# Attention and a gated feed-forward on one core: the high by high score products of two banks in the two halves of TensorE's rows

## The chip, the cores and the metric

The program runs on one core of a Trainium2 chip. The time is that of the device in microseconds for one execution of the whole program. A core has five engines that run their own queues: PE (TensorE, matmuls; its weight loads are shown apart as PEld), DVE (VectorE), ACT (ScalarE), POOL (GpSimd) and SP (SyncE, which here only issues DMAs). Matmuls write to banks of a separate memory (PSUM); one bank holds 512 columns of 32 bit for 128 rows.

## The reference

For 8 batches of 8 heads, 576 positions and 64 elements a head:

```python
scores = scale * np.matmul(q, k.transpose(0, 1, 3, 2))
cum = np.cumsum(np.maximum(s, 0.0), axis=-1)
bias = -(cum[:, :, :, None] - cum[:, :, None, :])
scores = np.where(causal, -1000000000.0, scores + np.minimum(bias, 0.0))
attn = softmax(scores)                      # with 1e-9 added to the sum
attn_out = np.matmul(attn, v)               # -> x: 4608 tokens x 512
gate = 1.0 / (1.0 + np.exp(-(x @ w_gate)))  # 512 x 1536
out = (gate * (x @ w_val)) @ w_out          # 1536 x 512
```

All inputs are 32 bit. The 64 (batch, head) pairs are called heads 0 to 63 below.

## The kernel before

**Split operands.** From head 8 on, and in the whole feed-forward, a 32 bit operand is split into a 16 bit high part and a 16 bit low part, and a product is made of matmuls of the parts. In the feed-forward that is three matmuls (high by high, high by low, low by high). Heads 0 to 7 are done with 32 bit matmuls (`n_prep`, `n_s`, `n_av`, `n_x`); these also contain the only matmuls of 64 rows, the transposes of a 64-row tile in `n_x` (line 628).

**The tile T of a head.** A head has 64 elements, so the two parts of q or k fill the 128 rows together. `split_qk` splits q and k, and one transposing DMA (line 394) writes `T[i]`, three planes of 576 columns: plane 0 has k's high part in rows 0 to 63 and its low part in rows 64 to 127, plane 1 the same of q. `swap_k` fills plane 2 by two DMAs on SP (lines 399 and 400): k's parts with the halves exchanged, low above and high below. There are three such tiles in turn.

**Scores.** A head's queries are cut into five tiles (`TILES`): tile 0 of 64 queries and tiles 1 to 4 of 128, which see 64, 192, 320, 448 and 576 keys. `s_part(i, t)` makes one tile's scores. Tile 4 takes two banks of 288 columns, the others one each: six banks a head. Per bank there are two matmuls of 128 rows with the same stationary operand, q's high and low part of the tile: with plane 0 (line 445) they give high by high plus low by low, with plane 2 (line 446) high by low plus low by high. `score_bank` gives out three banks in turn. DVE empties a bank in `max_part` (line 470, which adds the bias and takes the row minimum of the negated scores), ACT takes the exponential (line 473); POOL masks the bias row ahead of that (line 460).

**After the scores.** `p_part` splits the probabilities, a transposing DMA on SP turns them (line 493), `av_part` multiplies them by v, 40 matmuls a head of 64 or 65 columns (lines 505 to 510), two heads later; `x_part` and `split_x` make x of it, in 16 bit parts.

**The feed-forward.** It goes in 18 groups of 256 tokens by 12 blocks of 128 hidden columns. `ffn_in` makes one block: 24 matmuls of 256 columns (line 656; 48 smaller ones where the group lies across two batches). `ffn_out` adds it to the output: 6 matmuls of 512 columns (line 686).

**What sets the order.** A loop over ticks, five per head, calls these functions; a tick t of head i makes the scores of tile 4 - t, the mask and maximum of the tile before, and so on, and feed-forward blocks are set between by a quota. A scheduler that simulates the program's time then chooses the order of the instructions on each engine from this, the dependencies and the free buffers; some instructions (`pin`) are kept in the order in which they are written. From tick 90 on (head 18), `more_room` hands a large tile `t2big`, which shows as `t2f` in the profile, to a third T, second buffers for q and k and other things, under names in `spare`.

Of the kernel before, what the change touches and what calls it, by code (L numbers as in the profile page):

```python
# [7 lines left out]
F16 = mybir.dt.float16  # L8
# [8 lines left out]
P = 128  # L17
# [6 lines left out]
def tile_attention_then_gated_ffn(  # L24
# [11 lines left out]
    nc = tc.nc  # L36
    B, H, S, D = q.shape
# [7 lines left out]
    QC = S // QP  # L45

    TILES = [(0, 64, 64)] + [(64 + 128 * i, 128, 192 + 128 * i) for i in range(4)]
    NTL = len(TILES)
# [3 lines left out]
    PAD = NTL * P - S  # L52
# [11 lines left out]
    def score_bank(name):  # L64
        score["n"] += 1
        tag, bufs = ("x", 1) if score["n"] % 3 == 0 else ("s", 2)
        return pp.tile([P, 512], F32, tag=tag, name=name, bufs=bufs)
# [46 lines left out]
    def pin(ins):  # L114

        return tc.keep_in_program_order(ins) if spare else ins

    def first(now=True):
        return tc.high_priority(1000) if now else ExitStack()
# [84 lines left out]
    spare = {}  # L204

    def more_room():
        c = 0
        for name, n in (("qk16", QC * 2 * D), ("qk32", 4 * QC * D), ("T", 3 * S // 2), ("vsq0", S), ("vsq1", S)):
            spare[name] = t2big[:, c : c + n]
            c += n  # L210

# [2 lines left out]
    flat = w2all.rearrange("p f l n -> p (f l n)").bitcast(I32)  # L214
# [118 lines left out]
            out_scale(b)  # L333


    qk32, qkc, T, crow, v32, v16, vx, PT, xq, S_ps, rl, AV = {}, {}, {}, {}, {}, {}, {}, {}, {}, {}, {}, {}
    NG = (NT + GT - 1) // GT

    def load_qk(p):
# [58 lines left out]
    def swap_k(i):  # L398
        pin(nc.sync.dma_start(T[i][0:64, 2], T[i][64:128, 0]))
        pin(nc.sync.dma_start(T[i][64:128, 2], T[i][0:64, 0]))  # L400

    def load_crow(i):
        crow[i] = wp.tile([P, S], F32, tag="cr", name=f"cr{i}")
        if i > 0:
            nc.sync.dma_start(crow[i][0:1], cum_d[i : i + 1, :])
# [17 lines left out]
    def split_v(p):  # L423

        sc = sv[2 * p // H][0]
        t = wp.tile([P, 5, 2, 2 * D + 2], F16, tag="v16", name=f"v16_{p}")
        nc.gpsimd.memset(t[:, :, :, 2 * D :], 1.0)
        src = v32[p][:, :, :, 0:D]
        nc.scalar.activation(t[:, :, :, D : 2 * D], src, AF.Copy, scale=sc)
        nc.vector.scalar_tensor_tensor(t[:, :, :, 0:D], src, sc, t[:, :, :, D : 2 * D], ALU.mult, ALU.subtract)  # L430
        v16[p] = t

        vx[p] = v32[p].rearrange("p c h n -> p (c h n)").bitcast(F16).rearrange("p (c h n) -> p c h n", c=5, h=2)
        for g in range(2):
            nc.sync.dma_start(vx[p][64 * g : 64 * g + 64], t[:64])

    def s_part(i, t):
        w = TILES[t][2]
        c0 = S + t * P - PAD
        lhs = T[i].rearrange("p a n -> p (a n)")[:, c0 : c0 + P]  # L440
        pieces = [(0, w)] if w <= 512 else [(0, w // 2), (w // 2, w)]
        S_ps[i, t] = []
        for a, b_ in pieces:
            ps = score_bank(f"s{i}_{t}_{a}")
            nc.tensor.matmul(ps[:, : b_ - a], lhs, T[i][:, 0, a:b_], start=True, stop=False)  # L445
            nc.tensor.matmul(ps[:, : b_ - a], lhs, T[i][:, 2, a:b_], start=False, stop=True)  # L446
            S_ps[i, t].append((ps, a, b_))

    def bias_row(i):
        if i < NN:  # L450
            rl[i] = crow[i]
            return
        r = wp.tile([P, S], F32, tag="rl", name=f"rl{i}")
        nc.vector.tensor_scalar(r, crow[i], qkc[i // 2][1][:, 0:1], None, ALU.mult)
        rl[i] = r
# [112 lines left out]
    def n_s(i, t):  # L568
        q0, m, w = TILES[t]
        p, j = divmod(i, 2)  # L570
        nS[i, t] = []
        for a, b_ in [(0, w)] if w <= 512 else [(0, w // 2), (w // 2, w)]:
            ps = score_bank(f"s{i}_{t}_{a}")
            nc.tensor.matmul(ps[:, : b_ - a], qT[i][:, q0 : q0 + P], kT[p][:, a:b_], start=True, stop=True)
            nS[i, t].append((ps, a, b_))
# [146 lines left out]
    NE, NOFF = 44, 87  # L722
# [6 lines left out]
    for n in range(nticks + 12):  # L729
        if n == NTL * EARLY:  # L730
            more_room()
        i, t = divmod(n, NTL)
        if i < NN:
            with first():
                n_s(i, NTL - 1 - t)
                if t == 0:
                    bias_row(i)
        elif n < nticks:
            if t == 0:
                bias_row(i)  # L740
            with first(NE <= n < NOFF):
                s_part(i, NTL - 1 - t)
        if 2 <= n < nticks + 2:
            a, z = divmod(n - 2, NTL)
            if a < NN:
# [4 lines left out]
        if 1 <= n < nticks + 1:  # L750
            a, z = divmod(n - 1, NTL)
# [7 lines left out]
        if 3 <= n < 3 + NTL * NN:  # L759
            with first():  # L760
                a, z = divmod(n - 3, NTL)
# [11 lines left out]
        if i < NH:  # L773
            p, j = divmod(i, 2)
# [19 lines left out]
            if NN <= i and j == 0 and t == 0:  # L794
                split_v(p)
            if not spare:
# [9 lines left out]
                if t == 3 and NN - 1 <= i:  # L806
                    swap_k(i + 1)
            elif i <= EARLY + 1:
                if j == 0:
                    if t == 1:  # L810
                        split_qk(i + 1)
                    if t == 3:
                        swap_k(i + 1)
                        load_qk(p + 2)
                else:
                    if t == 0:
                        qk_square(p + 1)
                    if t == 1:
                        qk_scale(p + 1)
                    if t == 2:  # L820
                        split_qk(i + 1)
                    if t == 4:
                        swap_k(i + 1)
                        split_qk(i + 2)
                        load_qk(p + 3)
# [50 lines left out]
        if n >= NE and state["u"] < 2 * NF:  # L876
            fdone = min(NF, int((n - NE + 1) * FPT))
            while state["u"] < 2 * fdone:
                f = state["u"]
# [58 lines left out]
```

## Time and profile before

| | |
|---|---|
| median of 3 runs | 1164.59 us (1159.92 to 1169.75) |
| the profiled execution | 1161.21 us, of which the span from first to last instruction is 1159.4 us |
| PE | 1095.0 us busy, 11644 instructions |
| DVE, ACT, POOL | 775.0, 749.2 and 264.9 us busy |
| mean granted clock of PE | 0.979 |
| DMA | 157.62 MB, mean 136 GB/s |
| score matmuls of heads 8 to 63 start | from 110.8 to 973.4 us |
| head 19 starts its scores at | 285.1 us |

Times in rows of the profile are microseconds from the start of the span, durations of a single instruction in ns where the row says so. A row of the timeline has start, duration, engine, line, operation, names, the rows and columns of TensorE that a matmul uses (128\*128), the shape that it writes, the type and the count; neighbours of one line are merged into one row, which shows the form of the first. PE is the matmul side; the records of its matmuls overlap, since they are pipelined, so a matmul's duration is longer than the distance to the next one's start. `gv` and `o` are the feed-forward's banks, `s` the scores', `av` the attention output's, `na_ps`, `nt_ps`, `nx_ps`, `nq_ps` those of heads 0 to 7.

### The profile page before, as it was taken

What the parts mean: (1) busy time and instruction counts of PE and PEld (TensorE: products, weight loads), DVE (VectorE), ACT (ScalarE), POOL (GpSimd) and SP (SyncE); (2) the same over time, 40 slices, a digit from 0 to 9 for tenths busy, and PEclk for the clock granted to TensorE, in tenths of its full rate; (3) what the DMA queues carried; (4) which work ended last, traced back from release to release, by engine and by line L of the source; (5) the groups of instructions that cost most, each with busy time, mean ns of one, the idle gap of its engine ahead of it and who ended that gap; (6) DMA issues with size and microseconds to landing.
All of it is one profiled execution on the core that took longest, in us unless ns stands there. A gap on an engine that the chain in (4) does not pass through costs nothing.

```text
span 1159.4 us, 30337 instructions
## 1 busy us (share of the span) xinstructions
PE 1095.0 (94%) x11644; PEld 855.9 (74%) x11644; DVE 775.0 (67%) x2393; ACT 749.2 (65%) x1465; POOL 264.9 (23%) x570
## 2 busy tenths in 40 slices
PE   6786789989999999999999999999999999999997
PEld 5664677656777887778777777778877887787775
DVE  6888879785788777776566577777777775222221
ACT  6988667776777877676656577667777764233222
POOL 5535333231222222121111122222222221000000
PEclk9879899999999999999999999999999999999999
DMA  9675678898889797886737578877877764000000
GB/s 276 199 223 141 129 152 167 177 186 160 154 164 193 151 187 157 153 160 115 164 66 150 99 159 167 168 152 164 154 160 145 146 122 88 12 20 19 1 19 19
DMA packets 435886, 157.62 MB, mean 136 GB/s; under 512 B 403551, under 2 KB 423007, under 8 KB 435742
## 3 DMA queue, kind: packets, MB, share of 16 engines
q1 hardware_dynamic: 418398, 127.12, 57.1%
q10 hardware_dynamic: 13824, 16.78, 4.6%
q0 software_dynamic: 3520, 11.80, 3.1%
q8 instruction: 91, 1.49, 0.5%
q14 instruction: 53, 0.43, 0.1%
HBM read 56.92 MB, written 9.58 MB: 57 GB/s over the span
## 4 chain that ended last, share of the span: by engine, by line
PE 60%; issue 23%; DMA 5%; DVE 4%; ACT 3%; POOL 3%; SPq 1%; ACTq 0%; POOLq 0%; DVEq 0%
PE gv L656 33%; PE o L686 16%; PE s L446 3%; PE s L445 3%; DMA pt<-p 1%; PE av L505 1%; PE av L507 1%; PE av L506 1%; DMA T<-T 1%; POOL rl L460 1%; DMA T<-qk 1%; POOL cr L460 1%; PE na_ps L604 1%; DVE e L470 1%; DMA nqk<-in_q_dram 1%
## 5 line engine op out<-in xcount | busy, mean ns | idle before, releaser
L656 PE MATMUL gv<-x,w 128*128 128x256 f16 (+3 forms) x6912 | 614.9, 247 | 3.9 <-DVE t2f L663 2.3
L656 PEld LDWEIGHTS <-w 128*128 128x128 f16 x6912 | 535.1, 98 | 61.4 <-issue 4.6
L686 PE MATMUL o<-w2all,h 128*128 128x512 f16 x1296 | 314.8, 379 | 0.0
L460 POOL TENSOR_SCALAR_AFFINE_SELECT rl<-rl 128x64 f32<-128x64 f32 (+1 forms) x280 | 113.7, 407 | 512.0 <-DVE em L470 453.3
L473 ACT ACTIVATE e<-e,em 128x576 f32<-128x576 f32 x280 | 154.4, 554 | 88.0 <-DVE em L470 85.9
L661 ACT ACTIVATE th<-gv,scb 128x256 f32<-128x256 f32 (+3 forms) x288 | 111.3, 411 | 147.5 <-PE gv L656 142.5
L686 PEld LDWEIGHTS <-h 128*128 128x128 f16 x1296 | 123.4, 98 | 106.4
L663 DVE SCALAR_TENSOR_TENSOR t<-th,gv 128x256 f32<-128x256 f32 x192 | 80.0, 417 | 133.1 <-ACT th L661 131.9
L470 DVE CUSTOM_DVE_ANT_0 e<-s,rl,qkcf 128x288 f32<-128x288 f32 x280 | 135.7, 485 | 32.1 <-PE s L446 27.8
L671 ACT ACTIVATE h<-t,hsc 128x256 f16<-128x256 f32 x192 | 96.6, 503 | 80.4 <-DVE t L663 80.3
L482 DVE SCALAR_TENSOR_TENSOR p<-e,p 128x384 f16<-128x384 f32 x224 | 102.6, 498 | 41.0 <-ACT p L477 40.2
L672 DVE SCALAR_TENSOR_TENSOR h<-t,hsc,h 128x256 f16<-128x256 f32 x192 | 93.3, 486 | 43.4 <-ACT h L671 42.6
L477 ACT ACTIVATE p<-e 128x1152 f16<-128x1152 f32 x112 | 112.0, 1000 | 2.5
L505 PE MATMUL av<-v,pt 128*128 128x65 f16 x560 | 67.8, 193 | 5.3 <-DMA pt<-p 5.3
L446 PE MATMUL s<-T 128*128 128x288 f16 (+2 forms) x246 | 62.1, 279 | 11.3 <-DMA T<-T 11.3
L445 PE MATMUL s<-T 128*128 128x288 f16 (+2 forms) x246 | 64.4, 279 | 7.1 <-DMA T<-qk 4.2
L694 POOL DMA_DIRECT2D out_dram<-osb x36 | 20.4, 566 | 211.5 <-ACT osb L693 210.9
L507 PE MATMUL av<-v,pt 128*128 128x65 f16 x560 | 67.8, 194 | 0.0
L506 PE MATMUL av<-v,pt 128*128 128x64 f16 x560 | 67.7, 192 | 0.0
L505 PEld LDWEIGHTS <-pt 128*128 128x128 f16 x560 | 52.5, 98 | 11.0 <-DMA pt<-p 6.1
L408 POOL PARTITION_BROADCAST cr<-cr x63 | 58.5, 929 | 2.1 <-DMA cr<-cum_d 2.0
L506 PEld LDWEIGHTS <-pt 128*128 128x128 f16 x560 | 52.5, 97 | 4.9
(155 smaller groups left out, 1415.0 us busy)
## 6 DMA issues: line engine op xcount, KB each, us to landing
out_dram<-osb POOLq DMA_DIRECT2D x36, 256.0 KB, 2.8
v<-v SPq DMA_DIRECT2D x56, 162.5 KB
v<-in_v_dram SPq DMA_DIRECT2D x64, 128.0 KB
T<-T SPq DMA_DIRECT2D x82, 72.0 KB
t2f<-in_v_dram SPq DMA_DIRECT2D x20, 288.0 KB
qk<-in_q_dram SPq DMA_DIRECT2D x17, 288.0 KB
qk<-in_k_dram SPq DMA_DIRECT2D x17, 288.0 KB
w2all<-in_moe_w_gate_dram ACTq DMA_DIRECT2D x7, 512.0 KB
```

What stands on the lines that cost most here:

```text
L445: nc.tensor.matmul(ps[:, : b_ - a], lhs, T[i][:, 0, a:b_], start=True, stop=False)
L446: nc.tensor.matmul(ps[:, : b_ - a], lhs, T[i][:, 2, a:b_], start=False, stop=True)
L460: nc.gpsimd.affine_select(rl[i][:, q0:w], rl[i][:, q0:w], pattern=[[-1, m]], compare_op=ALU.is_ge, fill=-MASKED if i < NN else MASKED, bas ...
L470: nc.vector.tensor_tensor_reduce(e_t[t][:, a:b_], ps[:, : b_ - a], rl[i][:, a:b_], c, init, ALU.add, ALU.min, acc)
L473: nc.scalar.activation(e_t[t][:, :w], e_t[t][:, :w], AF.Exp, bias=init, scale=-1.0)
L477: nc.scalar.activation(p_s[h_][:, 0], e_s[h_], AF.Copy, scale=PSCALE)
L482: nc.vector.scalar_tensor_tensor(flat[:, LOW[t] * P : (LOW[t] + t) * P], e_t[t][:, : t * P], PSCALE, flat[:, kb * P : (kb + t) * P], ALU.m ...
L505: nc.tensor.matmul(AV[i][:, t], hi, v_[:, D : 2 * D + 1], start=kb == 0, stop=False)
L506: nc.tensor.matmul(AV[i][:, t, 0:D], hi, v_[:, 0:D], start=False, stop=False)
L656: nc.tensor.matmul(ps[:, gv, a:e], w1[f][:, cc, gv, wl], x_of(b, cc)[:, xl, c0 + a : c0 + e], start=(c == 0), stop=(c == 3 * NC - 1))
L661: nc.scalar.activation(th[:, a:e], ps[:, 0, a:e], AF.Tanh, scale=scb[b][:, f : f + 1])
L686: nc.tensor.matmul(ps[:m], h[:, hl, tt * P : tt * P + m], w2[f][:, wl], start=(f == 0 and c == 0), stop=(f == NF - 1 and c == 2))
```

## The change

From head 19 on (the first whose `swap_k` runs after `more_room`), the scores are made by a new function `s_pair` for two banks at a time.

* `swap_k` issues a third DMA on SP: it copies q's high part, plane 1 of rows 0 to 63 with the 64 columns before it (640 columns), to rows 64 to 127 of a tile `QD`, one of three in turn in `t2big`.
* `s_pair` takes two banks. The first gets high by high from rows 0 to 63 alone (q's high part and plane 0), the second from rows 64 to 127 alone (`QD` and plane 2, where k's high part lies below): two matmuls of 64 rows. Then each bank gets one matmul of 128 rows with plane 2, high by low plus low by high. The product low by low is left out for these heads. The number of matmuls stays at two per bank.
* The pairs are tile 4's two banks at tick 0 of a head, tiles 3 and 2 at tick 1, tiles 1 and 0 at tick 3. Mask and maximum keep their ticks.

```diff
-        for name, n in (("qk16", QC * 2 * D), ("qk32", 4 * QC * D), ("T", 3 * S // 2), ("vsq0", S), ("vsq1", S)):
+        for name, n in (("qk16", QC * 2 * D), ("qk32", 4 * QC * D), ("T", 3 * S // 2), ("vsq0", S), ("vsq1", S),
+                        ("qd0", NTL * P // 2), ("qd1", NTL * P // 2), ("qd2", NTL * P // 2)):
             spare[name] = t2big[:, c : c + n]
...
     def swap_k(i):
         pin(nc.sync.dma_start(T[i][0:64, 2], T[i][64:128, 0]))
         pin(nc.sync.dma_start(T[i][64:128, 2], T[i][0:64, 0]))
+        if spare:
+            QD[i] = spare[f"qd{i % 3}"].bitcast(F16)
+            pin(nc.sync.dma_start(QD[i][64:128], T[i].rearrange("p a n -> p (a n)")[0:64, S - PAD : 2 * S]))
...
+    def s_pair(i, tiles):
+
+        flat = T[i].rearrange("p a n -> p (a n)")
+        parts = []
+        for t in tiles:
+            w = TILES[t][2]
+            S_ps[i, t] = []
+            for a, b_ in [(0, w)] if w <= 512 else [(0, w // 2), (w // 2, w)]:
+                ps = score_bank(f"s{i}_{t}_{a}")
+                S_ps[i, t].append((ps, a, b_))
+                parts.append((t, ps, a, b_))
+        for g, (t, ps, a, b_) in enumerate(parts):
+            rows = slice(64 * g, 64 * g + 64)
+            lhs = QD[i][rows, t * P : (t + 1) * P] if g else flat[rows, S + t * P - PAD : S + (t + 1) * P - PAD]
+            nc.tensor.matmul(ps[:, : b_ - a], lhs, T[i][rows, 2 * g, a:b_], start=True, stop=False)
+        for t, ps, a, b_ in parts:
+            nc.tensor.matmul(ps[:, : b_ - a], flat[:, S + t * P - PAD : S + (t + 1) * P - PAD], T[i][:, 2, a:b_],
+                             start=False, stop=True)
...
-            with first(NE <= n < NOFF):
-                s_part(i, NTL - 1 - t)
+            if i not in QD:
+                with first(NE <= n < NOFF):
+                    s_part(i, NTL - 1 - t)
+            elif t in (0, 1, 3):
+                s_pair(i, {0: (4,), 1: (3, 2), 3: (1, 0)}[t])
```

In the changed kernel the 64-row matmul of `s_pair` is line 455 and the 128-row one line 457; the lines of the feed-forward are 679 and 709, of the value matmuls 528 and on. Three places of the order follow. In the names, `s45_4_288` is head 45's bank of tile 4 that starts at key 288, `t2f` holds QD.

PE, tile 4 of head 45, before:

```order
L686 MATMUL o9_1_11644<-w2all_78,h9_4_11707 128x512
L445 LDWEIGHTS T45_11591
L445 MATMUL s45_4_0_11981<-T45_11591 128x288
L446 LDWEIGHTS T45_11591
L446 MATMUL s45_4_0_11981<-T45_11591 128x288
L445 LDWEIGHTS T45_11591
L445 MATMUL s45_4_288_11984<-T45_11591 128x288
L446 LDWEIGHTS T45_11591
L446 MATMUL s45_4_288_11984<-T45_11591 128x288
L656 LDWEIGHTS w1_8_74
```

and now:

```order
L709 MATMUL o9_1_11670<-w2all_78,h9_4_11734 128x512
L455 LDWEIGHTS T45_11620
L455 MATMUL s45_4_0_12009<-T45_11620 128x288
L455 LDWEIGHTS t2f_135
L455 MATMUL s45_4_288_12010<-T45_11620,t2f_135 128x288
L457 LDWEIGHTS T45_11620
L457 MATMUL s45_4_0_12009<-T45_11620 128x288
L457 LDWEIGHTS T45_11620
L457 MATMUL s45_4_288_12010<-T45_11620 128x288
L679 LDWEIGHTS w1_8_74
```

The two first matmuls of the two banks now stand together as 64-row ones, between the same neighbours. PE, tiles 3 and 2 of head 45, before:

```order
L445 MATMUL s45_3_0_12034<-T45_11591 128x448
L446 LDWEIGHTS T45_11591
L446 MATMUL s45_3_0_12034<-T45_11591 128x448
L505 LDWEIGHTS pt1_43_11655
L505 MATMUL av43_12052<-v16_21_11212,pt1_43_11655 128x65
```

and now:

```order
L455 MATMUL s45_3_0_12062<-T45_11620 128x448
L455 LDWEIGHTS t2f_135
L455 MATMUL s45_2_0_12063<-T45_11620,t2f_135 128x320
L457 LDWEIGHTS T45_11620
L457 MATMUL s45_3_0_12062<-T45_11620 128x448
L457 LDWEIGHTS T45_11620
L457 MATMUL s45_2_0_12063<-T45_11620 128x320
L528 LDWEIGHTS pt1_43_11684
L528 MATMUL av43_12083<-v16_21_11237,pt1_43_11684 128x65
```

Tile 2, which stood behind the 40 value matmuls, now stands ahead of them beside tile 3. SP's queue around the swap for head 46, before:

```order
L394 DMA_TRANSPOSE T46_11874<-qk16_46_11869 128x12x96
L346 DMA t2f_135<-in_k_dram 96x12x64
L160 DMA t2f_135<-in_v_dram 128x576
L399 DMA T46_11874<-T46_11874 64x576
L400 DMA T46_11874<-T46_11874 64x576
L493 DMA_TRANSPOSE pt0_44_12042<-p16_0_81 128x9x128
```

and now:

```order
L395 DMA_TRANSPOSE T46_11901<-qk16_46_11896 128x12x96
L347 DMA t2f_135<-in_k_dram 96x12x64
L160 DMA t2f_135<-in_v_dram 128x576
L400 DMA T46_11901<-T46_11901 64x576
L401 DMA T46_11901<-T46_11901 64x576
L404 DMA t2f_135<-T46_11901 64x640
L516 DMA_TRANSPOSE pt0_44_12073<-p16_0_81 128x9x128
```

The copy to QD (L404) goes out behind the two swaps and ahead of the transpose of the probabilities of head 44; the rest of the queue keeps its order here.

More of the change, by code (lines that the diff above doesn't have):

```diff
@@ L333, in ffn_scale @@
             out_scale(b)
-    qk32, qkc, T, crow, v32, v16, vx, PT, xq, S_ps, rl, AV = {}, {}, {}, {}, {}, {}, {}, {}, {}, {}, {}, {}
+    qk32, qkc, T, crow, QD, v32, v16, vx, PT, xq, S_ps, rl, AV = {}, {}, {}, {}, {}, {}, {}, {}, {}, {}, {}, {}, {}
     NG = (NT + GT - 1) // GT
```

## The prediction

> **What bounds the kernel now.** I read the page first, then the windows, then the waits, then PE's own timeline in a head of the middle stretch.
>
> ```profile
> span 1159.4 us, 30337 instructions
> PE 1095.0 (94%) x11644; PEld 855.9 (74%) x11644; DVE 775.0 (67%) x2393; ACT 749.2 (65%) x1465; POOL 264.9 (23%) x570
> ...
> 270.00:390.00 120.00, 115.46 (x1417) 91.22 (x1416) 91.01 (x298) 86.35 (x175) 30.77 (x69) 1.00 0.84 166
> 390.00:974.00 584.00, 584.00 (x6803) 462.21 (x6801) 420.51 (x1366) 403.78 (x791) 125.23 (x301) 1.00 0.74 145
> 974.00:1159.00 185.00, 178.84 (x1702) 136.62 (x1700) 44.10 (x104) 52.69 (x113) 4.83 (x9) 0.99 0.08 20
> ```
>
> The last three rows are stretches: start and end, length, then busy time of PE, PEld, DVE, ACT and POOL, the granted clock, the DMA share and GB/s. PE is busy in all 584 us from 390 to 974 and in 115.46 of the 120 us before; the clock is full in both. Heads 19 to 63, the ones that change, have their score matmuls inside these two stretches. Of the other engines none is over 76% busy there (DVE, 91.01 of 120 us). So in this part a microsecond more on PE is a microsecond more of span, and one less is one less, but for 4.5 us of PE idle between 270 and 390, of which these waits are the most:
>
> ```profile
> PE s L446 <- DMA t2f<-t2f: 1.9, 1, 1.9
> PE s L446 <- DMA T<-T: 1.3, 1, 1.3
> PE s L445 <- DMA t2f<-qk: 0.9, 1, 0.9
> ```
>
> (Waiter, awaited, us in total, times, longest.) A busy PE says nothing of what one matmul costs, since they are pipelined; a matmul costs the time from its start to the next one's. For head 45:
>
> ```profile
> 703.83 0.29 PE L445 MATMUL s<-T 128*128 128x288 f16 x1
> 703.95 0.29 PE L446 MATMUL s<-T 128*128 128x288 f16 x1
> ...
> 704.32 2.78 PE L656 MATMUL gv<-x,w 128*128 128x256 f16 x24
> ...
> 708.23 0.35 PE L445 MATMUL s<-T 128*128 128x448 f16 x1
> 708.42 0.35 PE L446 MATMUL s<-T 128*128 128x448 f16 x1
> 709.82 0.30 PE L445 MATMUL s<-T 128*128 128x320 f16 x1
> 709.95 0.30 PE L446 MATMUL s<-T 128*128 128x320 f16 x1
> 710.09 2.78 PE L656 MATMUL gv<-x,w 128*128 128x256 f16 x24
> ...
> 714.00 0.25 PE L445 MATMUL s<-T 128*128 128x192 f16 x1
> ...
> 714.17 0.19 PE L445 MATMUL s<-T 128*128 128x64 f16 x1
> 714.20 0.19 PE L446 MATMUL s<-T 128*128 128x64 f16 x1
> ...
> 718.14 0.29 PE L445 MATMUL s<-T 128*128 128x288 f16 x1
> ```
>
> One of 288 columns costs 0.122 us (0.49 for four), of 448 0.19, of 320 0.135 (0.27 for two), of 192 0.085, of 64 0.03. Nothing waits; the next head starts 14.3 us later.
>
> **What the side-by-side halves save.** Before, two banks take four full matmuls. After, they take two of 64 rows, which use different rows of the array and different banks, and two full ones; the number of matmuls is the same. If the two halves run at the same time, a pair saves the shorter of its two: 0.122 in tile 4, 0.135 for tiles 3 and 2, 0.03 for tiles 1 and 0, together 0.287 us a head. The order of the changed program does not pair all of them. Counted over the whole of it, 40 pairs of 288 and 288, 38 of 448 and 320 and 43 of 192 and 64 stand back to back; 26 halves stand alone (18 in heads 19 to 24, 8 as tiles 3 and 2 of heads 26, 34, 50 and 58), and two halves in the same rows stand together once. What stands alone costs as much as the full matmul it replaces, since cost goes by columns. Saved: 40 x 0.122 + 38 x 0.135 + 43 x 0.03 = 4.9 + 5.1 + 1.3 = 11.3 us. No row of this trace has two 64-row matmuls in different halves, so the bounds are 11.3 (side by side) and 0 (one after the other). I take 11.3: no semaphore stands between the two and neither rows nor banks are shared.
>
> The Trainium skill ("TensorE: Matmul & The Clock Gate", part 3 on packing small matmuls) says that matmuls on distinct row groups start about 4 ns apart and run concurrently. No run here shows it yet.
>
> **What going into 64 rows and out again costs.** This is the term that decides. The kernel has four matmuls of 64 rows, the transposes of a 64-row tile (L628), among matmuls of 128 rows. Two of the four places, PE and then the weight loads:
>
> ```profile
> 76.13 0.50 PE L595 MATMUL nt_ps<-ident,e 128*128 128x128 f32 x3
> 76.46 1.00 PE L604 MATMUL na_ps<-v,p 128*128 128x65 f32 x8
> 77.19 0.28 PE L604 MATMUL na_ps<-v,p 128*128 128x65 f32 x1
> 77.40 0.64 PE L628 MATMUL nx_ps<-ident,nx 64*128 64x64 f32 x3
> 77.87 0.41 PE L557 MATMUL nq_ps<-ident,nqk 96*128 96x96 f32 x3
> 78.12 0.58 PE L604 MATMUL na_ps<-v,p 128*128 128x65 f32 x4
> ...
> 107.93 0.50 PE L595 MATMUL nt_ps<-ident,e 128*128 128x128 f32 x3
> 108.36 0.64 PE L628 MATMUL nx_ps<-ident,nx 64*128 64x64 f32 x3
> 108.83 0.33 PE L574 MATMUL s<-nk,nq 128*128 128x64 f32 x2
> ...
> 77.39 0.14 PEld L628 LDWEIGHTS nx_ps<-ident,nx 64*128 64x128 f32 x1
> 77.60 0.20 PEld L628 LDWEIGHTS nx_ps<-ident,nx 128*128 128x128 f32 x2
> ```
>
> Rows of one line are merged; the form shown is the first one's. (77.19 is the last of the eight from 76.46.) Three 128-column transposes of full rows take 0.33 us (76.13 to 76.46), 0.11 each. The group of L628 is one of 64 rows and 64 columns and two full ones: by columns it should take 0.055 + 0.22 = 0.275 us. It takes 0.47 in both places (77.40 to 77.87, 108.36 to 108.83): 0.195 too much. And it starts late: 0.21 after the last matmul before it (77.19) instead of about 0.11, and 0.43 after the start of three transposes (107.93) instead of 0.33: another 0.10. Its weights are loaded only at its own start (77.39), and the next full ones' only 0.2 us later (77.60), where elsewhere loads run ahead under the matmul before. So one excursion into 64 rows and back costs 0.10 + 0.195 = about 0.30 us. The 96-row transposes right behind it (77.87 to 78.12, 0.083 each) show no such gap: it is not the number of rows as such, but the 64-row tile.
>
> The Trainium skill ("TensorEngine Tiling (Array Packing)", key properties) says that a change of tiling mode, not of the tile alone, drains TensorE; it gives no length. The trace agrees, with 0.30 us there and back. This rule speaks against the change.
>
> For 16 bit operands a part of the 0.30 is smaller, the loads that stand open:
>
> ```profile
> L628 PEld LDWEIGHTS nx_ps<-ident,nx 64*128 64x128 f32 x1 | 0.1, 135 | 0.1
> L445 PEld LDWEIGHTS <-T 128*128 128x128 f16 x246 | 24.1, 98 | 19.0 <-DMA T<-qk 5.6
> ```
>
> A load is 135 ns there and 98 ns for scores (the mean, behind the busy time). Two open loads make 0.30 - 2 x 0.037 = 0.225; I take 0.22 us. The bounds: 0.30, all as in the 32 bit rows, and 0.195, as if one way cost nothing more. In the changed order PE goes into 64 rows 148 times (121 pairs, the mixed one, 26 alone). 148 x 0.22 = 32.6 us; bounds 28.9 and 44.4.
>
> **The rest of the change.** The order of tiles: tile 2 moves up beside tile 3, ahead of the 40 value matmuls, and tile 0 beside 1. A pair wants two banks at once, so PE may wait for DVE, which empties them; behind it would queue the feed-forward matmuls.
>
> ```profile
> 709.04 0.68 DVE L470 CUSTOM_DVE_ANT_0 e<-s,rl,qkcf 128x448 f32<-128x448 f32 x1
> 715.08 0.41 DVE L470 CUSTOM_DVE_ANT_0 e<-s,rl,qkcf 128x192 f32<-128x192 f32 x1
> ```
>
> With three banks in turn, tiles 1 and 0 (714.00) need tile 3's bank, emptied at 709.72, and the next head's tile 4 (718.14) needs tile 1's, emptied at 715.49: 4.3 and 2.6 us to spare. Cost nothing; without that cover, up to 0.68 us a pair.
>
> The copy of q's high part is 45 more DMAs, each on SP behind the two swaps:
>
> ```profile
> 704.55 0.47 SPq L399 DMA_DIRECT2D T<-T  x1
> 705.07 0.59 SPq L400 DMA_DIRECT2D T<-T  x1
> 705.83 1.31 SPq L493 DMA_TRANSPOSE pt<-p  x1
> ...
> 351.44 3.36 DMA T<-T
> ```
>
> A third issue like the second (0.59 us) would go out at 705.7 and land some 3.4 us later (the swap in the chain of waits), near 709.1; its head reads it at 718.14. The transpose behind it moves by 0.6 us and is needed for the value matmuls a head later. So it costs nothing in the middle. In heads 19 to 24, where PE waits for swaps now, it is between +3.6 us (six heads, 0.6 later each) and -4.5 us (the present idle takes up some of the added PE time). I take 0. ACT, DVE and POOL get no instruction more.
>
> **The sum.** -11.3 + 32.6 = +21.3 us. On the profiled execution (span 1159.4, time 1161.2) that is 1182.5; the median of the runs is 3.4 us above it, 1164.6, and gives 1185.9. I say 1185. The forecast's own range: +28.9 - 11.3 - 4.5 = +13.1 to +44.4 - 11.3 + 3.6 = +36.7, that is 1174 (low end, on the profiled execution) to 1201 (high end, on the median).
>
> **The rivals.** *Faster: 16 bit pays no switch.* Loads of 16 bit weights into the other tile run ahead as they do everywhere else, and only the 11.3 us are left: 1150 to 1153. The trace's four excursions are all of 32 bit, which speaks for it being possible; that the wait stands in the matmul's own start as well as in the load speaks against. It decides below 11.3 / 148 = 0.076 us an excursion. Chance 0.08. The Trainium skill's tiling page gives row tiling with two tiles up to 2x (theoretical speedup), which is this case. *A cheap switch* of 0.08 to 0.15 us, half of what the rows show: +0.5 to +10.9 us, 1165 to 1176. Chance 0.13. *It does not do what it says:* the halves run one after the other. Nothing saved: +28.9 to +44.4, 1194 to 1209, most likely 1197. Chance 0.12; no row speaks for it or against. The forecast has 0.67.
>
> The bound for a difference is 1%, 11.6 us; the three runs before are 0.85% apart. Faster 0.05 (most of the first rival), same 0.17 (the cheap switch and the rest of the first), slower 0.78. The range that leaves out the first rival, the lower half of the cheap switch and the top of the third is 1168 to 1207.
>
> **What would show it.** In the profile after: the time from the start of a score pair's first matmul in heads 27 to 63 to that of the feed-forward matmul behind it, now 0.49 us for tile 4, should be about 0.49 - 0.12 + 0.22 = 0.59, counted from the end of the stream before it; the head's period should go from 14.3 to about 14.7 us; the second half should start within some tens of ns of the first (if 0.12 us later, the third rival); the weight load of the first full matmul should start only after the halves have gone through, 0.1 us or more (if it starts with them, the first rival). PE should be as busy in its stretch, and the time from 974 to the end, with no scores in it, unchanged at 185 us. I am wrong if the period stays at 14.3 or falls, or if PE waits for banks or for the copy.

## The result and the profile after

The changed kernel takes 1184.8 us (median of 4 runs, 1177.14 to 1187.89) against 1167.17 us before (4 runs): a ratio of 1.015, 95% interval 1.0102 to 1.0197, so 12 to 23 us slower. 1185 was forecast, and slower by over 1%.

The page after, and two stretches, from the start of head 19's scores to the last scores and from there to the end:

```profile
span 1185.8 us, 30440 instructions
PE 1115.8 (94%) x11644; PEld 836.2 (71%) x11644; DVE 774.5 (65%) x2393; ACT 747.5 (63%) x1465; POOL 265.8 (22%) x570
...
292.80:1000.00 707.20, 703.83 (x8010) 522.23 (x8008) 502.36 (x1638) 478.70 (x945) 152.05 (x362) 1.00 0.77 150
1000.00:1186.00 186.00, 179.18 (x1706) 136.96 (x1703) 44.32 (x104) 52.90 (x114) 4.78 (x9) 0.99 0.07 20
```

PE is as full as before (703.83 of 707.20 us), DVE, ACT and POOL do the same work, and the feed-forward's tail after the last scores is unchanged at 186 us. So the time went into what PE does in heads 19 to 63. Where these start and how they follow, first before, then after:

```profile
285.10 0.29 PE L445 MATMUL s<-T 128*128 128x288 f16 x1
397.81 0.29 PE L445 MATMUL s<-T 128*128 128x288 f16 x1
...
292.84 0.29 PE L455 MATMUL s<-T 64*128 64x288 f16 x1
408.44 0.29 PE L455 MATMUL s<-T 64*128 64x288 f16 x1
```

These are the first score matmuls of heads 19 and 27. From head 19's to the end of the span it is 874.3 us before and 893.0 after: 18.7 us more. The other 7.7 us between the two profiled executions lie ahead of head 19, up to which PE's order of instructions is the same in both. They are variation from run to run: in the nine profiles of this study head 19 starts anywhere from 283.0 us (same_rows, below) to 295.3 (alone_64), and among these the three kernels without a copy to QD start it at 285.10 (before), 287.96 (alone_96) and 295.29 (alone_64).

Head 45 on PE: first the row ahead of its tile 4 before, then the rows after, with the weight loads of tile 4 (these answer to the rows from 703.83 on before):

```profile
702.53 1.46 PE L686 MATMUL o<-w2all,h 128*128 128x512 f16 x6
...
721.64 1.46 PE L709 MATMUL o<-w2all,h 128*128 128x512 f16 x6
723.03 0.29 PE L455 MATMUL s<-T 64*128 64x288 f16 x1
723.03 0.29 PE L455 MATMUL s<-T,t2f 64*128 64x288 f16 x1
723.26 0.42 PE L457 MATMUL s<-T 128*128 128x288 f16 x2
723.51 2.78 PE L679 MATMUL gv<-x,w 128*128 128x256 f16 x24
...
727.52 0.36 PE L455 MATMUL s<-T 64*128 64x448 f16 x1
727.53 0.31 PE L455 MATMUL s<-T,t2f 64*128 64x320 f16 x1
727.82 0.50 PE L457 MATMUL s<-T 128*128 128x448 f16 x2
...
733.38 0.25 PE L455 MATMUL s<-T 64*128 64x192 f16 x1
733.38 0.20 PE L455 MATMUL s<-T,t2f 64*128 64x64 f16 x1
733.56 0.28 PE L457 MATMUL s<-T 128*128 128x192 f16 x2
733.68 2.78 PE L679 MATMUL gv<-x,w 128*128 128x256 f16 x24
...
737.70 0.29 PE L455 MATMUL s<-T 64*128 64x288 f16 x1
...
723.02 0.09 PEld L455 LDWEIGHTS <-T 64*128 64x128 f16 x1 [0.42 <-issue]
723.03 0.09 PEld L455 LDWEIGHTS <-t2f 64*128 64x128 f16 x1
723.25 0.11 PEld L457 LDWEIGHTS <-T 128*128 128x128 f16 x2
```

The two halves of a pair start together. But the first starts 0.09 us late: six matmuls of 512 columns take 1.30 us (702.53 to 703.83 before), which ends at 722.94, and the halves start at 723.03. The full ones follow 0.23 us after the halves (723.26), where 288 columns take 0.12: 0.11 late. The two full ones then take 0.25 us (723.26 to 723.51) where two took 0.24 before: another 0.01. The weight loads show the same: those of the halves and of the full matmuls stand only at their own start, and not under the matmul before. The head lasts 14.67 us (723.03 to 737.70), against 14.32 before (703.83 to 718.14, which are rounded), 0.35 us more. "Busy" shows none of this, since a matmul's record runs on past its stream and covers the gap.

### The profile page after: what moved, and what is told of

Same layout as the page of the kernel before. It is cut to its first block, busy times and chain, and to the rows that moved or that the text cites. A ratio compares the mean times of both kernels' runs of the same rounds, so it can differ in the third digit from the quotient of the medians.

```text
span 1185.8 us, 30440 instructions
## 1 busy us (share of the span) xinstructions
PE 1115.8 (94%) x11644; PEld 836.2 (71%) x11644; DVE 774.5 (65%) x2393; ACT 747.5 (63%) x1465; POOL 265.8 (22%) x570
## 4 chain that ended last, share of the span: by engine, by line
PE 59%; issue 21%; DMA 7%; ACT 4%; DVE 4%; POOL 2%; SPq 2%; ACTq 0%; POOLq 0%; DVEq 0%
PE gv L679 31%; PE o L709 16%; PE s L457 4%; PE s L455 2%; DMA T<-qk 2%; DMA v<-in_v_dram 1%; DMA pt<-p 1%; PE av L528 1%; PE av L530 1%; PE av L529 1%; PE s L597 1%; POOL rl L483 1%; DVE e L493 1%; ACT w L292 1%; ACT e L609 1%
## 5 line engine op out<-in xcount | busy, mean ns | idle before, releaser
L493 DVE CUSTOM_DVE_ANT_0 e<-s,rl,qkcf 128x288 f32<-128x288 f32 x280 | 135.8, 485 | 36.3 <-PE s L469 12.7
L528 PEld LDWEIGHTS <-pt 128*128 128x128 f16 x560 | 52.5, 98 | 9.1 <-DMA pt<-p 4.7
L477 DVE TENSOR_SCALAR rl<-cr,qkcf 128x576 f32<-128x576 f32 x56 | 29.2, 521 | 42.9 <-POOL cr L412 42.6
L529 PEld LDWEIGHTS <-pt 128*128 128x128 f16 x560 | 52.5, 97 | 2.7
L530 PEld LDWEIGHTS <-pt 128*128 128x128 f16 x560 | 52.7, 97 | 0.4 <-issue 0.3
```

The source lines that it names most:

```text
L493: nc.vector.tensor_tensor_reduce(e_t[t][:, a:b_], ps[:, : b_ - a], rl[i][:, a:b_], c, init, ALU.add, ALU.min, acc)
L528: nc.tensor.matmul(AV[i][:, t], hi, v_[:, D : 2 * D + 1], start=kb == 0, stop=False)
L529: nc.tensor.matmul(AV[i][:, t, 0:D], hi, v_[:, 0:D], start=False, stop=False)
L530: nc.tensor.matmul(AV[i][:, t], lo, v_[:, D : 2 * D + 1], start=False, stop=False)
```

## The experiments

All are read by the head's period, the time from head 45's first matmul of tile 4 to head 46's, in a stretch where PE never waits. It repeats to 0.01 or 0.02 us, while whole times of one kernel differ by up to 1.4% (order_full, ten runs: 1158.95 to 1175.06 us).

**order_full.** The change without its 64-row matmuls:

```diff
-        for g, (t, ps, a, b_) in enumerate(parts):
-            rows = slice(64 * g, 64 * g + 64)
-            lhs = QD[i][rows, t * P : (t + 1) * P] if g else flat[rows, S + t * P - PAD : S + (t + 1) * P - PAD]
-            nc.tensor.matmul(ps[:, : b_ - a], lhs, T[i][rows, 2 * g, a:b_], start=True, stop=False)
+        for t, ps, a, b_ in parts:
+            lhs = flat[:, S + t * P - PAD : S + (t + 1) * P - PAD]
+            nc.tensor.matmul(ps[:, : b_ - a], lhs, T[i][:, 0, a:b_], start=True, stop=False)
```

> The changed kernel with its copy to QD, its pairs and its order, but the first matmul of each bank is one of 128 rows again (plane 0, so low by low is computed again) and QD is never read. Theory: the whole loss is the way into 64 rows and back, about 0.21 us an excursion (0.63 us a head) less 0.287 us that the halves save. With neither, the head's period in the stretches of 256-column feed-forward matmuls is 14.32 us as before, not 14.66, and the time is that of before within 0.5%. Rival: the loss is the price of two banks at once, of tile 2 ahead of the value matmuls, or of the third DMA: then the period stays near 14.66 us or above.

```profile
716.89 0.29 PE L454 MATMUL s<-T 128*128 128x288 f16 x1
...
731.21 0.29 PE L454 MATMUL s<-T 128*128 128x288 f16 x1
```

Period 14.32 us; the time is 1.0013 times that of before (95% interval 0.9975 to 1.0051). The copy, the pairs and the order of tiles are not the loss. They are not quite free either: see the waits for banks in the next section.

**same_rows.** Both halves in rows 0 to 63:

```diff
-        for g, (t, ps, a, b_) in enumerate(parts):
-            rows = slice(64 * g, 64 * g + 64)
-            lhs = QD[i][rows, t * P : (t + 1) * P] if g else flat[rows, S + t * P - PAD : S + (t + 1) * P - PAD]
-            nc.tensor.matmul(ps[:, : b_ - a], lhs, T[i][rows, 2 * g, a:b_], start=True, stop=False)
+        for t, ps, a, b_ in parts:
+            lhs = flat[0:64, S + t * P - PAD : S + (t + 1) * P - PAD]
+            nc.tensor.matmul(ps[:, : b_ - a], lhs, T[i][0:64, 0, a:b_], start=True, stop=False)
```

> The changed kernel with both halves of a pair in rows 0 to 63, so QD is never read; low by low is left out as in the changed kernel. Theory: in the changed kernel the halves run side by side, and the excursion costs the same whichever rows it uses. In the same rows they must follow one another, so a head loses the 0.287 us that the change saves: period 14.95 us, some 11 to 13 us above the changed kernel. Rival: the halves save nothing in the changed kernel either (they only start together in the records): period 14.66 us.

```profile
716.87 0.41 PE L454 MATMUL s<-T 64*128 64x288 f16 x2
717.22 0.30 PE L456 MATMUL s<-T 128*128 128x288 f16 x1
...
731.81 0.29 PE L454 MATMUL s<-T 64*128 64x288 f16 x1
```

The full matmuls now come 0.35 us after the first half instead of 0.23, and the period is 14.94: 0.28 more than the changed kernel's 14.67. That is what the halves save by running side by side, and it shows that they do. The whole time, 1186.71 us in its one run, is only 2 us above the changed kernel's median and not the 11 to 13 expected: this run started head 19 at 283.0 us and the profiled one of the changed kernel at 292.84. From head 19 to the last score matmul it is 715.7 us, against 706.9 for the changed kernel: 8.8 more. The whole time of a single run decides nothing of this size here.

**alone_64 and alone_96.** The kernel before, with fewer rows in the first matmul of each bank from head 19 on (64 or 96):

```diff
-            nc.tensor.matmul(ps[:, : b_ - a], lhs, T[i][:, 0, a:b_], start=True, stop=False)
+            r = slice(0, 64 if i > EARLY else P)
+            nc.tensor.matmul(ps[:, : b_ - a], lhs[r], T[i][r, 0, a:b_], start=True, stop=False)
```

> The kernel before, but from head 19 on the first matmul of every bank uses rows 0 to 63 alone (high by high; low by low is left out), the second all 128, in the old order: six excursions a head that save nothing, 268 in all. Theory: 0.21 us each, whatever stands around: period 14.32 + 6 x 0.21 = 15.58 us, +56 us in all, about 1223. Rival: the cost is that of the second half's rows, of QD or of pairs, not of the switch: period 14.32 and the time of before.

> As alone_64, but the first matmul of every bank uses rows 0 to 95 (high by high and half of low by low; the other half is left out). Theory: it is the 64-row tile that TensorE has to empty itself for, not that rows are left unused or that two neighbours use different rows: period 14.32 us and the time of before. Rival: any matmul with other rows than its neighbour's pays: period near 15.58 us.

Head 45's tile 4 and the start of head 46, with 64 rows and then with 96:

```profile
743.13 0.29 PE L446 MATMUL s<-T 64*128 64x288 f16 x1
743.36 0.30 PE L447 MATMUL s<-T 128*128 128x288 f16 x1
743.59 0.29 PE L446 MATMUL s<-T 64*128 64x288 f16 x1
743.81 0.30 PE L447 MATMUL s<-T 128*128 128x288 f16 x1
...
758.70 0.29 PE L446 MATMUL s<-T 64*128 64x288 f16 x1
...
710.20 0.29 PE L446 MATMUL s<-T 96*128 96x288 f16 x1
710.33 0.29 PE L447 MATMUL s<-T 128*128 128x288 f16 x1
710.45 0.29 PE L446 MATMUL s<-T 96*128 96x288 f16 x1
710.58 0.29 PE L447 MATMUL s<-T 128*128 128x288 f16 x1
...
724.54 0.29 PE L446 MATMUL s<-T 96*128 96x288 f16 x1
```

With 64 rows every step between the two kinds takes 0.22 to 0.23 us instead of 0.12; the period is 15.57 and the time 1224.28 us, as forecast. (15.57 - 14.32) / 6 = 0.208 us an excursion. With 96 rows the steps are 0.12 to 0.13, the period is 14.34 and the time 1168.1 us. So the cost is that of going between the 64-row tile and the full array, both ways; it needs no second half, no QD and no pair, and rows left unused do not cause it.

**no_10.** The changed kernel with tiles 1 and 0 as before the change:

```diff
-            elif t in (0, 1, 3):
-                s_pair(i, {0: (4,), 1: (3, 2), 3: (1, 0)}[t])
+            elif t in (0, 1):
+                s_pair(i, {0: (4,), 1: (3, 2)}[t])
+            elif t in (3, 4):
+                s_part(i, NTL - 1 - t)
```

> The changed kernel, but tiles 1 and 0 are made as before, by two matmuls of 128 rows a bank at ticks 3 and 4 (with low by low). Two excursions a head instead of three, 103 in all. Theory: an excursion costs 0.21 us whatever its width, and this one saved only 0.03, so the head's period falls from 14.66 us by 0.18 to 14.48, and the time by some 8 us. Rival: what an excursion costs goes with its columns (0.627 us a head over 1600 columns): then the 256 columns of tiles 1 and 0 bring only 0.07 us, period 14.59.

```profile
718.60 0.29 PE L455 MATMUL s<-T 64*128 64x288 f16 x1
...
733.08 0.29 PE L455 MATMUL s<-T 64*128 64x288 f16 x1
```

Period 14.48 us, as the theory had it; by columns it would have been 14.59. The time is 1179.68 us in one run, against 1164.52 before beside it. That is 5 us under the changed kernel's median, where some 8 were expected; a single run does not tell 5 from 8.

**wide_full and wide_half.** Tile 4's two banks 512 columns wide, with full first matmuls and with halves; the other tiles as before the change:

```diff
+    def s_wide(i):
...
+        banks = [score_bank(f"s{i}_4_{a}") for a in (0, 288)]
+        S_ps[i, 4] = [(banks[0], 0, 288), (banks[1][:, 224:512], 288, 576)]
+        q_ = flat[:, S + 4 * P - PAD : S + 5 * P - PAD]
+        for g, ps in enumerate(banks):
+            nc.tensor.matmul(ps, q_, T[i][:, 0, 64 * g : 64 * g + 512], start=True, stop=False)
+        for g, ps in enumerate(banks):
+            nc.tensor.matmul(ps, q_, T[i][:, 2, 64 * g : 64 * g + 512], start=False, stop=True)
...
-            elif t in (0, 1, 3):
-                s_pair(i, {0: (4,), 1: (3, 2), 3: (1, 0)}[t])
+            elif t == 0:
+                s_wide(i)
+            else:
+                s_part(i, NTL - 1 - t)
```

and from the first to the second:

```diff
-            nc.tensor.matmul(ps, q_, T[i][:, 0, 64 * g : 64 * g + 512], start=True, stop=False)
+            rows = slice(64 * g, 64 * g + 64)
+            lhs = QD[i][rows, 4 * P : 5 * P] if g else q_[rows]
+            nc.tensor.matmul(ps, lhs, T[i][rows, 2 * g, 64 * g : 64 * g + 512], start=True, stop=False)
```

> The base of wide_half. From head 19 on tile 4's two banks are each computed 512 columns wide instead of 288 (keys 0 to 511 and 64 to 575; the extra columns are not read), by two matmuls of 128 rows; tiles 3 to 0 as before the change; the copy to QD stays, unread. Theory and rival alike: four matmuls of 0.216 instead of 0.122 us, so the period is 14.32 + 0.38 = 14.70 us.

> wide_full with the first matmuls of the two banks as halves of 64 rows side by side, 512 columns each (low by low of tile 4 is left out): one excursion a head. Theory: it saves one matmul of 512 columns, 0.215 us, and costs 0.21, so the period is that of wide_full within 0.02 us: about 510 columns are where a pair breaks even. Rival: the cost grows with the columns in the array (0.21 at 288, 0.37 at 512): period 0.16 us above wide_full, and no width pays.

PE from the last feed-forward matmul ahead of tile 4 to the first behind it, wide_full and then wide_half:

```profile
714.84 0.38 PE L720 MATMUL o<-w2all,h 128*128 128x512 f16 x1
715.06 0.38 PE L467 MATMUL s<-T 128*128 128x512 f16 x1
715.92 0.71 PE L690 MATMUL gv<-x,w 128*128 128x256 f16 x5
...
715.27 0.38 PE L722 MATMUL o<-w2all,h 128*128 128x512 f16 x1
715.59 0.39 PE L469 MATMUL s<-T 64*128 64x512 f16 x1
715.59 0.39 PE L469 MATMUL s<-T,t2f 64*128 64x512 f16 x1
716.35 0.49 PE L692 MATMUL gv<-x,w 128*128 128x256 f16 x3
```

Both take 1.08 us from row to row; the periods are 14.69 and 14.69 us, the times 1179.85 and 1179.91. A full-width bank of 512 columns is where a pair of halves breaks even: it saves one matmul of 0.215 us and pays one excursion. The cost does not grow with the columns: to 0.01 us it is the same at 512 as at the 64 to 448 of the other runs.

## Why the prediction was right, and where it was off

**What bounds the kernel.** Right: PE stayed full, and what the period lost, the span lost.

**What the halves save.** Right at its upper bound. They start together in the records and same_rows loses 0.28 us a head without that (0.287 forecast). The rival in which they run one after the other has fallen. The sentence of the Trainium skill ("TensorE: Matmul & The Clock Gate", part 3) on matmuls of distinct row groups running concurrently, about 4 ns apart, agrees with this trace, where both halves stand at 723.03 us.

**What an excursion costs.** The deciding term, 0.22 us, was right in kind and 5% too large. Four kernels give it by the period: the changed one (14.67 - 14.32 + 0.287) / 3 = 0.212, alone_64 0.208, no_10 (14.48 - 14.32 + 0.257) / 2 = 0.21, and wide_half, where it equals 0.215 within 0.01; 0.21 is used below.

The step from the 32 bit transposes of heads 0 to 7 (0.30 us) to 16 bit came out in its total, but not in the way it was worked out, and that is in part luck. It took 0.037 us off each of two open weight loads, one on the way in and one on the way out, which leaves 0.10 - 0.037 = 0.06 us in and 0.195 - 0.037 = 0.16 out. Head 45 shows 0.09 in and 0.11 + 0.01 = 0.12 out. The way in is thus nearly as long as in the 32 bit rows, and almost all of the difference is on the way out; the two errors cancel. Why the way out is shorter for 16 bit by more than one load's 0.037 us stays open.

So the rival in which 16 bit operands pay no switch has fallen, and the cheap switch too. The Trainium skill's rule ("TensorEngine Tiling (Array Packing)", key properties) that a change of tiling mode drains TensorE agrees; the "up to 2x" that the same page gives as a theoretical speedup for two row tiles is not reached by pairs this short between full matmuls, where 448 and 320 columns saved 0.135 us and paid 0.21.

**The sum.** 148 excursions x 0.21 - 11.3 = +19.8 us, where 21.3 was forecast. 18.7 was measured from head 19 on. The rest is PE's idle time, in the stretch from head 19 to head 27, before and then after, and in that from head 27 to the last scores after (length, then PE's busy time; before, PE had no idle time from 390 to 974 us):

```profile
285.10:397.81 112.71, 108.17 (x1320) 85.63 (x1319) 89.60 (x299) 84.20 (x169) 27.93 (x64) 1.00 0.86 168
...
292.84:408.44 115.60, 113.67 (x1319) 83.40 (x1318) 88.57 (x298) 83.61 (x168) 26.90 (x64) 1.00 0.88 169
408.44:1000.00 591.56, 590.12 (x6692) 438.82 (x6692) 413.75 (x1340) 395.09 (x778) 125.15 (x298) 1.00 0.75 146
```

From head 19 to head 27 the idle time falls from 4.5 to 1.9 us: 2.6 us of the added work went into waits that had been there, within the -4.5 to +3.6 that the prediction gave and set to 0. From head 27 on it rises from nothing to 1.4 us, which are the waits of the next paragraph. 19.8 - 2.6 + 1.4 = 18.6 us. That the median of the whole times, 1184.8 us, stands 0.2 us from the 1185 of the forecast is luck: the four runs behind it lie 11 us apart.

**Two banks at once.** This step failed: I put its cost at nothing, by 2.6 us and more to spare in head 45, and I worked that out for two of the three pairs only. In the third, tiles 3 and 2, the half of tile 2 needs the bank of tile 4's first 288 columns; in head 45 there was time to spare there too, since before the change DVE had emptied it at 704.86 and tile 3 started at 708.23:

```profile
704.35 0.51 DVE L470 CUSTOM_DVE_ANT_0 e<-s,rl,qkcf 128x288 f32<-128x288 f32 x1
```

In a few heads DVE is later than that. The waits of PE for DVE's bank from head 19 on: before, in the changed kernel and in order_full:

```profile
PE s L445 <- DVE em L470: 0.4, 2, 0.2
...
PE s L455 <- DVE em L493: 1.4, 2, 0.8
...
PE s L454 <- DVE em L492: 4.7, 5, 1.6
```

One of the two in the changed kernel, in head 28, on PE and on DVE:

```profile
427.84 0.36 PE L455 MATMUL s<-T 64*128 64x448 f16 x1
428.80 0.29 PE L455 MATMUL s<-T,t2f 64*128 64x320 f16 x1 [0.60 <-DVE em L493]
...
427.89 0.42 DVE L686 SCALAR_TENSOR_TENSOR t<-th,gv 128x256 f32<-128x256 f32 x1 [2.10 <-ACT th L684]
428.23 0.51 DVE L493 CUSTOM_DVE_ANT_0 e<-s,rl,qkcf 128x288 f32<-128x288 f32 x1
```

PE wants the bank that DVE's L493 is to empty; L493 stands in DVE's queue behind a feed-forward instruction that waited 2.10 us for ACT. The other, in head 32 (0.84 us), is like it: tile 2's 320 columns wait for tile 4's first 288. So both are in the pair that the prediction did not work out. A bank that is free in time in one head says nothing of the heads in which DVE itself waits for ACT. The cost was small, 1.4 us here. In order_full PE waits in the same two heads for longer, 0.94 and 1.62 us, and in three more, two of them at tile 2 again. Why the waits are longer there stays open.

**The copy.** Right: no wait for it in the middle stretch, one of 0.2 us in all.

## What to carry to other kernels

A matmul of 64 rows among matmuls of 128 pays for the way in and out; here that was 0.21 us an excursion, whatever its width, and two halves side by side saved only the shorter one's stream. So count excursions against columns: at 0.215 us for 512 columns, 0.21 us is by estimate the price of some 500, and a pair of two halves whose shorter one is narrower than that loses. Look for a price like this in the one odd corner of the program that already does the thing (here four transposes), and take it from start to start, since busy time hides it.

## What the runs showed of the hardware that I had not expected

Matmuls of 96 rows between full ones cost next to nothing (0.02 us a head for six), and one pays for the 64-row tile by its size alone: 64 rows of the same tile T, in the same places, cost 1.25 us a head. The excursion's price split almost evenly between the way in (0.09 us) and the way out (0.12). A version faster than both kernels was not found: a bank has 512 columns, at which a pair only breaks even, and an excursion with four halves was not tried.
